# RWKV recurrence and MoE block: weight staging in one tile, and low parts and two products moved to GpSimd

## The chip, the core and the metric

One core of one Trainium2 chip runs the whole kernel in one launch. The metric is the device time of an execution in microseconds (us), shown as the median of several runs. Beside the runs stands one profiled execution of the kernel, from which all durations below are taken.

## What is computed

The reference runs a linear recurrence over 768 time steps for 4 x 8 heads of width 40, and then a two-layer block over the 3072 tokens that come out of it:

```python
for t in range(S):
    y[:, :, t] = einsum('bhd,bhde->bhe', rt, state)
    Sa = einsum('bhde,bhe->bhd', state, at)
    state = state * wt[:, :, None, :] - einsum('bhd,bhe->bhde', Sa, bt)
    state = state + einsum('bhd,bhe->bhde', vt, kt)
x = y.transpose(0, 2, 1, 3).reshape(B * S, H * D)      # 3072 x 320
h = x @ w_in                                           # 320 x 2048
g = where(h >= 1, h, where(h <= -1, 0, (h + 1) ** 2 / 4))
out = g @ w_out                                        # 2048 x 320
```

All inputs and outputs are fp32.

## The kernel before

**The recurrence.** Time is cut into 24 chunks of 32 steps, and six sets of four chunks. Per set the kernel forms the running products of w, their reciprocals (`rec`), and from them a, b and k scaled by these; it stores the scaled rows to a scratch in DRAM and reads them back per chunk in another layout. Each chunk has a 32 x 32 triangular matrix per head; its inverse is made for a whole set at a time by 31 elimination steps of two instructions each (`invert`, L362 and L368). Set 0's steps run on VectorE, those of the later sets on GpSimd. With the inverse at hand, `chain` carries the state from chunk to chunk through a fixed series: products on TensorE (L516, L526, L542, L553, L582), small scalings of their results on VectorE (L533, L560, L565, L584) and copies out of PSUM on ScalarE (L520, L537, L547).

**The start.** Sets 0 and 1 are prepared by `early_rows` (L164 to L193). For set 1 the inputs w, a, b and k are loaded early into tiles that later serve other ends: w into X0, a into X1, b into `tiab`, k into Y. X0 and X1 are also the tiles in which the tokens of the two-layer block will stand (in rows, X and X_92, X_93). `early_turn` transposes the rows of `at` (j = 0) and then of `bt` (j = 1) on TensorE in four parts each, `early_evict` copies them out of PSUM on ScalarE (L216), and `early_ab` (L227) makes the products from which set 1's triangular matrices come. PSUM has four rotating buffers for all of this and for the chain.

**The weights.** w_in comes as 12 pieces (jobs 0 to 11, tiles w_00 to w_32 of 120 or 80 rows by 512 columns), w_out as 16 pieces (128 x 320). They lie in DRAM as 8-byte words, of which this code rebuilds fp32 and splits it into a high and a low part. A job has these steps: raw loads queued on GpSimd (L708); two ScalarE passes, one that makes the upper bits in a place x (L720) and one that makes the lowest bits in a place `low` (L724); a VectorE pass that joins them in x (L728); then, one step later in the generator, the rounded high part on ScalarE (L740), and the low part as the difference of x and the high part (L741), on VectorE for w_in and on GpSimd for w_out. Each third piece of w_in also issues two copies on GpSimd (L746), and every split queues the raw load of five jobs on. x and `low` of the w_in jobs are thirds of X1 and of X0, taken in turn:

```python
x, low = (y[0:m, n * ((k + 1) % 3) :][:, 0:n] for y in (Xraw[1], Xraw[0]))
...
nc.scalar.copy(hi, x)
(nc.gpsimd if kind else nc.vector).tensor_sub(lo, x, hi.bitcast(F32))
```

**What sets the order.** The schedule is manual: each engine runs its instructions in the order in which the program text issues them, and the order is fixed by the code (`fill`, `feed`, `background`, and the list `steps` for set 1). An instruction that waits holds everything behind it on its engine. DMAs issued on SyncE and on GpSimd stand in these queues as well.

**The two-layer block** (`moe`) runs in twelve groups of 64 time steps as soon as `relayout` has moved the tokens from Y to X0 or X1 by DMA (L602 to L611). Per step: 16 products of 120 x 256 (L628), a gate (L636, L637 on ScalarE, L639 on VectorE), a split of the gate's result into a high part (L645, ScalarE) and a low part (L646, GpSimd), and 12 products (L658).

Of the kernel before, what the change touches and what calls it, by code (L numbers as in the profile page):

```python
# [9 lines left out]
F32 = mybir.dt.float32  # L10
# [44 lines left out]
def rwkv_moe_kernel(ctx: ExitStack, tc: tile.TileContext, r, k, v, w, a, b, w_in, w_out, ident_d, mask_d, out):  # L55
    nc = tc.nc
# [38 lines left out]
    Xraw = [x_tile(i, F32).rearrange("p c n -> p (c n)") for i in range(2)]  # L95
# [71 lines left out]
    def early_rows(s):  # L167


        wl, al, bl, kl = early_in[s]  # L170
        R = early_out[s]
        kt, P, at, bt = (R[:, :, D * i : D * i + D] for i in range(4))
        rec = arena[:, 0 : L * D].rearrange("p (t e) -> p t e", e=D)
        seg = lambda x: x.rearrange("p (s t) e -> p s t e", t=8)
        Ps, ws, rs = seg(P), seg(wl), seg(rec)
        nc.vector.tensor_copy(Ps[:, 1:, 0], ws[:, 1:, 0])
        nc.vector.tensor_scalar(out=P[:, 0], in0=wl[:, 0], scalar1=-1.0, scalar2=None, op0=ALU.mult)
        for t in range(1, 8):
            nc.vector.tensor_mul(Ps[:, :, t], Ps[:, :, t - 1], ws[:, :, t])
        for i in range(1, 4):  # L180
            nc.vector.tensor_mul(Ps[:, i], Ps[:, i], Ps[:, i - 1, 7:8].broadcast_to([128, 8, D]))
        yield
        nc.vector.tensor_scalar(out=at[:, 0], in0=al[:, 0], scalar1=-1.0, scalar2=None, op0=ALU.mult)
        nc.vector.tensor_mul(at[:, 1:], al[:, 1:], P[:, 0 : L - 1])
        yield
        nc.vector.reciprocal(rs[:, :, 7], Ps[:, :, 7])
        for t in range(7, 0, -1):
            nc.vector.tensor_mul(rs[:, :, t - 1], rs[:, :, t], ws[:, :, t])
        yield
        nc.vector.tensor_mul(bt, bl, rec)  # L190
        yield
        nc.vector.tensor_mul(kt, kl, rec)
        yield  # L193

    def early_turn(s, j, part):
# [499 lines left out]
    def weight_tile(k, t):  # L695
        kind, j, i, _ = jobs[k]
        if kind:
            if w2_pool[j // 8 ^ 1] is None:
                open_w2(j // 8 ^ 1)
            return w2_pool[j // 8 ^ 1].tile([128, 2, 320], t, name=f"w2_{j}", tag=f"w2_{j}")  # L700
        return w1_tile(j, i, t)

    def raw_load(k):
        raws[k] = weight_tile(k, F32).rearrange("p b n -> p (b n)")
        x, at = raws[k].bitcast(I32), 0
        for src in jobs[k][3]:
            m = src.shape[0]
            nc.gpsimd.dma_start(x[at : at + m], src.bitcast(I32))  # L708
            at += m

    def weights():

        def start(k):
            m, n = sizes[k]
            words = raws[k][0:m]
            if jobs[k][0]:
                x, low = Xraw[1][0:m, n * ((k + 2) % 3) :][:, 0:n], Xraw[1][0:m, 3 * n : 4 * n]
            else:
                x, low = (y[0:m, n * ((k + 1) % 3) :][:, 0:n] for y in (Xraw[1], Xraw[0]))
            nc.scalar.activation(  # L720
                x, words.rearrange("p (n b) -> p n b", b=2)[:, :, 1], AF.Prelu, scale=2.0**-112, alpha=2.0**32
            )
            low = low.bitcast(U32)
            nc.scalar.activation(  # L724
                low, words.bitcast(U8).rearrange("p (n b) -> p n b", b=8)[:, :, 3], AF.Copy, bias=-15.5 / 32, scale=1.0 / 32
            )
            yield
            nc.vector.scalar_tensor_tensor(  # L728
                out=x.bitcast(U32), in0=x.bitcast(U32), scalar=3, in1=low,
                op0=ALU.logical_shift_left, op1=ALU.bitwise_or,  # L730
            )
            yield x

        def split(k, x):
            m, n = sizes[k]
            kind, j, i, _ = jobs[k]
            del raws[k]
            wt[kind, j, i] = new = weight_tile(k, F32R)
            hi, lo = (new[0:m, p] for p in range(2))
            nc.scalar.copy(hi, x)  # L740
            (nc.gpsimd if kind else nc.vector).tensor_sub(lo, x, hi.bitcast(F32))  # L741
            converted[0] = k + 1
            if (kind, i) == (0, 2):
                wb = new.bitcast(F32)
                for q in range(2):
                    nc.gpsimd.dma_start(wb[80:120, q], wb[40 * q : 40 * q + 40, 0])  # L746
            if k + AHEAD < len(jobs):
                raw_load(k + AHEAD)

        late = None  # L750
        for k in range(len(jobs)):
            s = start(k)
            next(s)
            yield
            if late:
                split(*late)
            yield
            late = k, next(s)
            yield
        split(*late)  # L760

    def pull(gen, n=1):
# [25 lines left out]
    for i in range(2):  # L788
        init_cg(i, 2)
    rows_of = [early_rows(s) for s in range(2)]  # L790
    for j in range(2):
        for _ in range(2):
# [32 lines left out]
    i = 0  # L825
# [139 lines left out]
```

## Time and profile before

| | |
|---|---|
| runs, us | 864.71, 864.89, 858.93; median 864.71 |
| profiled execution, first to last instruction | 859.4 us |
| TensorE matmul busy | 690.8 us (80%) |
| VectorE busy | 594.3 us (69%) |
| ScalarE busy | 417.5 us (49%) |
| GpSimd busy | 441.8 us (51%) |
| moved by DMA | 122.01 MB |

The profiled execution lies between the runs: its span is 5.3 us under their median and 0.5 us over the fastest. In the rows, PE is the TensorE matmul, DVE is VectorE, ACT is ScalarE, POOL is GpSimd and SP is SyncE. L with a number is a line of the kernel. A letter q behind an engine (SPq) is its instruction queue. "x8" counts instructions that a row merges, and a square bracket tells how long the engine sat idle before the row and what ended that.

### The profile page before, as it was taken

What the parts mean: (1) busy time and instruction counts of PE and PEld (TensorE: products, weight loads), DVE (VectorE), ACT (ScalarE), POOL (GpSimd) and SP (SyncE); (2) the same over time, 40 slices, a digit from 0 to 9 for tenths busy, and PEclk for the clock granted to TensorE, in tenths of its full rate; (3) what the DMA queues carried; (4) which work ended last, traced back from release to release, by engine and by line L of the source; (5) the groups of instructions that cost most, each with busy time, mean ns of one, the idle gap of its engine ahead of it and who ended that gap; (6) DMA issues with size and microseconds to landing.
All of it is one profiled execution on the core that took longest, in us unless ns stands there. A gap on an engine that the chain in (4) does not pass through costs nothing.

```text
span 859.4 us, 35431 instructions
## 1 busy us (share of the span) xinstructions
PE 690.8 (80%) x15360; PEld 633.3 (74%) x15360; DVE 594.3 (69%) x1338; ACT 417.5 (49%) x888; POOL 441.8 (51%) x621
## 2 busy tenths in 40 slices
PE   4225656687567877878998889999999999999994
PEld 4224545576456866768887789898898999999994
DVE  6895689888556845787677797677876778676210
ACT  6306455557433533445545455455455555555552
POOL 0300279986232677845678548674267742222331
PEclk9665656788786989879999799999999999999998
DMA  8999599987598666986858976667354456350100
GB/s 291 188 198 233 95 194 206 217 196 184 130 172 149 152 156 112 181 189 150 165 127 165 190 179 154 131 130 134 85 111 89 98 106 131 84 119 23 36 16 16
DMA packets 221459, 122.01 MB, mean 142 GB/s; under 512 B 142144, under 2 KB 214016, under 8 KB 221304
## 3 DMA queue, kind: packets, MB, share of 16 engines
q1 hardware_dynamic: 215032, 98.12, 56.6%
q0 software_dynamic: 6272, 21.63, 9.4%
q8 instruction: 121, 1.98, 1.1%
q14 instruction: 34, 0.28, 0.1%
HBM read 90.54 MB, written 27.53 MB: 137 GB/s over the span
## 4 chain that ended last, share of the span: by engine, by line
PE 42%; DMA 10%; DVE 6%; POOL 5%; ACT 3%; SPq 3%; issue 2%; ACTq 0%; DVEq 0%; POOLq 0%
PE ph L628 14%; PE po L658 13%; PE p L553 4%; DMA ti<-scr 3%; PE p L542 3%; SPq L313 3%; DMA tiab<-scr 2%; PE p L516 2%; PE p L582 2%; PE p L482 2%; PE p L526 2%; DMA ld_b<-in_b_dram 2%; DMA scr<-arena 2%; POOL gl L646 1%; POOL lw L368 1%
## 5 line engine op out<-in xcount | busy, mean ns | idle before, releaser
L646 POOL TENSOR_TENSOR gl<-gt,gh 128x512 fp32r<-128x512 f32 x96 | 123.8, 1290 | 204.5 <-ACT gh L645 204.5
L628 PE MATMUL ph<-X,w 120*128 120x256 f32 x1536 | 219.1, 296 | 1.2 <-issue 1.2
L628 PEld LDWEIGHTS ph<-X,w 120*128 120x128 f32 x1536 | 198.7, 198 | 8.3 <-issue 1.7
L658 PE MATMUL po<-w,gh 128*128 128x320 f32 x768 | 135.9, 320 | 19.8 <-ACT gh L645 19.8
L658 PEld LDWEIGHTS po<-w,gh 128*128 128x128 f32 x768 | 117.4, 193 | 23.8 <-ACT gh L645 23.1
L639 DVE SCALAR_TENSOR_TENSOR gt<-gt,ph 128x512 f32<-128x512 f32 x96 | 65.7, 684 | 96.2 <-ACT gt L637 87.2
L537 ACT ACTIVATE cg<-p 32x160 f32<-32x160 f32 x192 | 56.5, 295 | 92.5 <-PE p L526 58.8
L658 PE MATMUL po<-w,gl 128*128 128x320 f32 x384 | 79.7, 332 | 20.7 <-POOL gl L646 20.7
L560 DVE SCALAR_TENSOR_TENSOR cg<-p,pr 40x160 f32<-40x160 f32 x184 | 59.1, 321 | 50.8 <-PE p L553 48.7
L636 ACT ACTIVATE gt<-ph,half_c 128x512 f32<-128x512 f32 x96 | 66.0, 688 | 58.0 <-PE ph L628 58.0
L368 POOL TENSOR_TENSOR lw<-lw 128x31 f32<-128x31 f32 (+15 forms) x155 | 86.6, 559 | 9.4
L362 POOL TENSOR_TENSOR lw<-lw 128x31 f32<-128x31 f32 (+15 forms) x155 | 84.0, 542 | 8.9
L494 DVE TENSOR_TENSOR cg<-p,mask 32x256 f32<-32x256 f32 x192 | 80.6, 420 | 3.5
L658 PEld LDWEIGHTS po<-w,gl 128*128 128x128 f32 x384 | 63.7, 201 | 25.3 <-POOL gl L646 24.9
L553 PE MATMUL p<-cg 128*64 128x72 f32 (+1 forms) x1536 | 66.0, 245 | 0.0
L645 ACT CAST gh<-gt 128x512 fp32r<-128x512 f32 x96 | 59.6, 621 | 10.5 <-DVE gt L639 9.5
L547 ACT COPY ss<-p 40x320 f32<-40x320 f32 x92 | 38.6, 419 | 48.7 <-PE p L542 47.2
L637 ACT ACTIVATE gt<-gt 128x512 f32<-128x512 f32 x96 | 60.7, 632 | 3.1
L553 PEld LDWEIGHTS p<-cg 128*64 128x64 f32 x1536 | 60.4, 154 | 0.4 <-issue 0.4
L533 DVE SCALAR_TENSOR_TENSOR cg<-p,mask 32x128 f32<-32x128 f32 x192 | 55.3, 288 | 6.3 <-PE p L526 1.1
L582 PEld LDWEIGHTS p<-pr,ss 40*40 40x40 f32 x1472 | 35.9, 129 | 30.1 <-issue 23.1
L582 PE MATMUL p<-pr,ss 40*40 40x32 f32 x1472 | 40.9, 210 | 21.1 <-DVE pr L466 16.3
(94 smaller groups left out, 1058.9 us busy)
## 6 DMA issues: line engine op xcount, KB each, us to landing
ti<-scr SPq DMA_DIRECT2D x96, 200.0 KB
ti<-scr SPq DMA_DIRECT2D x96, 168.0 KB
scr<-arena POOLq DMA_DIRECT2D x16, 640.0 KB, 6.4
cg<-scr SPq DMA_DIRECT2D x96, 80.0 KB
X<-Y SPq DMA_DIRECT2D x36, 160.0 KB
scr<-wide SPq DMA_DIRECT2D x8, 640.0 KB
w<-in_moe_w_out_dram POOLq DMA_DIRECT2D x16, 320.0 KB, 5.2
tiab<-scr SPq DMA_DIRECT2D x32, 160.0 KB
```

Of the source, the lines that this page charges most:

```text
L362: eng.tensor_mul(t3, W3[:, 0:n, j : j + 1].broadcast_to([128, n, m]), L3[:, j + 1 :, j].unsqueeze(1).broadcast_to([128, n, m]),)
L368: eng.tensor_sub(W3[:, 0:n, j + 1 :], W3[:, 0:n, j + 1 :], t3)
L494: nc.vector.tensor_tensor(out=cg[q, f::2, C_X : C_X + 64][:, 4 * i : 4 * i + 4].rearrange("p h (j x) -> p h j x", x=32), in0=ps[quarter(f, ...
L553: nc.tensor.matmul(psv[h // 8][64 * f : 64 * f + 64, h // 2 % 4, 0:n3], lhsT=cgw[:, h * CW + C_G : h * CW + C_G + 64], rhs=cg[:, h, C_R : ...
L582: nc.tensor.matmul(psv[er[f], p, :], lhsT=ss[er[f], p, :], rhs=pn[er[f], p, 0, 8:40], start=True, stop=True)
L628: nc.tensor.matmul(phs[k % 2][:, n * j : n * j + n], lhsT=wt[0, f // 4, wi // 2][:, wi % 2, fs], rhs=Xs[g][:, xi, :], start=i == 0, stop=i ...
L636: nc.scalar.activation(gt, ph, AF.Relu, bias=half_c, scale=0.5)
L637: nc.scalar.activation(gt, gt, AF.Square)
L639: nc.vector.scalar_tensor_tensor(out=gt, in0=gt, scalar=1.0, in1=ph, op0=ALU.min, op1=ALU.max)
L645: nc.scalar.copy(gh, gt)
L646: nc.gpsimd.tensor_sub(gl, gt, gh.bitcast(F32))
L658: nc.tensor.matmul(pos[i], lhsT=x[:, ts_], rhs=w, start=q == 0 and k == 0, stop=end)
```

## The change

Three edits. First, the products `bt` and `kt` of set 1 (and only of set 1) are formed by GpSimd. Second, the w_in jobs take both x and `low` from X1: x alternates between its first and second third, and `low` is always the last third; X0 is no longer used for weights. Third, the low part of all weights, w_in too, is formed by GpSimd.

```diff
@@ early_rows
-        nc.vector.tensor_mul(bt, bl, rec)
+        eng = nc.gpsimd if s else nc.vector
+        eng.tensor_mul(bt, bl, rec)
         yield
-        nc.vector.tensor_mul(kt, kl, rec)
+        eng.tensor_mul(kt, kl, rec)
         yield
@@ weights / start
-                x, low = (y[0:m, n * ((k + 1) % 3) :][:, 0:n] for y in (Xraw[1], Xraw[0]))
+                x, low = (Xraw[1][0:m, n * i : n * i + n] for i in ((k + 1) % 2, 2))
@@ weights / split
-            (nc.gpsimd if kind else nc.vector).tensor_sub(lo, x, hi.bitcast(F32))
+            nc.gpsimd.tensor_sub(lo, x, hi.bitcast(F32))
```

Behind L190 each line number of the changed kernel is higher by one. The order on TensorE and SyncE is the same in both kernels, and on ScalarE only the place of `low` differs. VectorE's order loses fourteen instructions and GpSimd's gains them.

VectorE where set 1's reciprocals end (L188), in the program before. X_93 is X1, X_92 is X0, wide_100 is the tile of set 1's rows, arena holds `rec`, w_00 and w_01 are the first two pieces of w_in, cg and p belong to the chain:

```order
L188 TENSOR_TENSOR arena<-arena,X_92 128x4x40 x7
L190 TENSOR_TENSOR wide_100<-tiab,arena 128x32x40
L728 SCALAR_TENSOR_TENSOR X_93<-X_93,X_92 120x512
L192 TENSOR_TENSOR wide_100<-Y,arena 128x32x40
L741 TENSOR_TENSOR w_00_732<-X_93,w_00_732 120x512
L533 SCALAR_TENSOR_TENSOR cg_85<-p_738,mask 32x4x32 x2
```

The same place in the changed program:

```order
L188 TENSOR_TENSOR arena<-arena,X_92 128x4x40 x7
L729 SCALAR_TENSOR_TENSOR X_93<-X_93 120x512
L534 SCALAR_TENSOR_TENSOR cg_85<-p_738,mask 32x4x32 x2
L534 SCALAR_TENSOR_TENSOR cg_85<-p_739,mask 32x4x32 x2
L495 TENSOR_TENSOR cg_86<-p_764,mask 32x4x64 x4
```

The two products and the first difference are gone from in front of the chain's L533 (now L534); only one joining pass is left between the reciprocals and the chain.

GpSimd behind the first raw loads, in the program before (pr_90 is a tile that is cleared once the transposes have read it):

```order
L708 DMA w_11_506<-in_moe_w_in_dram 40x1024
L708 DMA w_12_735<-in_moe_w_in_dram 40x1024 x2
L708 DMA w_20_959<-in_moe_w_in_dram 80x1024
L708 DMA w_20_959<-in_moe_w_in_dram 40x1024
L131 MEMSET pr_90 128x16x8
```

The same place in the changed program:

```order
L709 DMA w_11_506<-in_moe_w_in_dram 40x1024
L191 ISA
L191 TENSOR_TENSOR wide_100<-tiab,arena 128x32x40
L193 TENSOR_TENSOR wide_100<-Y,arena 128x32x40
L742 TENSOR_TENSOR w_00_732<-X_93,w_00_732 120x512
L709 DMA w_12_735<-in_moe_w_in_dram 40x1024 x2
L742 TENSOR_TENSOR w_01_956<-X_93,w_01_956 120x512
L709 DMA w_20_959<-in_moe_w_in_dram 80x1024
L709 DMA w_20_959<-in_moe_w_in_dram 40x1024
L131 MEMSET pr_90 128x16x8
```

The raw loads of w_12 and w_20 now stand behind the products and behind the first differences.

GpSimd amid set 1's elimination steps (tile lw), before:

```order
L573 TENSOR_TENSOR Y<-yt,Y 128x2x4x32
L362 TENSOR_TENSOR lw<-lw 128x156
L708 DMA w_32_1418<-in_moe_w_in_dram 40x1024 x2
L368 TENSOR_TENSOR lw<-lw 128x6x26
L362 TENSOR_TENSOR lw<-lw 128x175
L708 DMA w_0_1433<-in_moe_w_out_dram 128x640
L368 TENSOR_TENSOR lw<-lw 128x7x25
```

The same stretch in the changed program:

```order
L574 TENSOR_TENSOR Y<-yt,Y 128x2x4x32
L363 TENSOR_TENSOR lw<-lw 128x156
L742 TENSOR_TENSOR w_20_1415<-X_93,w_20_1415 120x512
L709 DMA w_32_1418<-in_moe_w_in_dram 40x1024 x2
L369 TENSOR_TENSOR lw<-lw 128x6x26
L363 TENSOR_TENSOR lw<-lw 128x175
L742 TENSOR_TENSOR w_21_1426<-X_93,w_21_1426 120x512
L709 DMA w_0_1433<-in_moe_w_out_dram 128x640
L369 TENSOR_TENSOR lw<-lw 128x7x25
```

Each difference of w_in stands ahead of the raw load that its split queues, between elimination steps.

## Rows read from the trace of the kernel before

**Rows 1.** Timeline of ACT, 47 to 84 us: start, us, instruction, idle before.

```profile
47.05 0.68 ACT L720 ACTIVATE X<-w 120x512 f32<-120x512 f32 x1
...
67.61 0.67 ACT L724 ACTIVATE X<-w 120x512 uint32<-120x512 uint8 x1 [19.89 <-DVE arena L188]
68.19 4.73 ACT L216 COPY wide<-p 40x512 f32<-40x512 f32 x8
...
82.80 1.18 ACT L216 COPY wide<-p 40x512 f32<-40x512 f32 x2
```

**Rows 2.** Timeline of DVE, 27 to 76 us.

```profile
27.68 1.45 DVE L184 TENSOR_TENSOR wide<-X,wide 128x1240 f32<-128x1240 f32 x1
...
65.10 2.48 DVE L188 TENSOR_TENSOR arena<-arena,X 128x160 f32<-128x160 f32 x7
67.62 1.49 DVE L190 TENSOR_TENSOR wide<-tiab,arena 128x1280 f32<-128x1280 f32 x1
69.03 0.69 DVE L728 SCALAR_TENSOR_TENSOR X<-X,X 120x512 uint32<-120x512 uint32 x1
...
74.72 0.69 DVE L741 TENSOR_TENSOR w<-X,w 120x512 fp32r<-120x512 f32 x1 [3.60 <-ACT w L740]
75.42 1.21 DVE L533 SCALAR_TENSOR_TENSOR cg<-p,mask 32x128 f32<-32x128 f32 x4
```

**Rows 3.** Windows: length, busy us (count) of each engine, clock, DMA share, GB/s.

```profile
82.90:97.25 14.35, 9.11 (x384) 8.36 (x384) 5.12 (x11) 5.90 (x12) 0.00 (x0) 0.64 0.28 30
...
111.52:145.38 33.86, 21.88 (x640) 19.70 (x632) 30.24 (x67) 18.07 (x43) 31.23 (x50) 0.60 1.08 191
145.38:163.22 17.84, 13.11 (x274) 11.71 (x266) 17.26 (x39) 11.70 (x28) 17.22 (x23) 0.80 0.98 218
```

**Rows 4.** Waits of 150 to 185 us: who waited for whom, total, times, longest.

```profile
PE po L658 <- POOL gl L646: 8.3, 2, 6.4
...
ACT arena L279 <- DMA scr<-arena: 4.9, 1, 4.9
```

**Rows 5.** Waits of SyncE's queue, 20 to 240 us.

```profile
SPq L602 <- POOL w L741: 7.3, 1, 7.3
```

**Rows 6.** Windows of 100 us.

```profile
500.00:600.00 100.00, 95.77 (x2333) 87.66 (x2332) 77.98 (x186) 51.92 (x116) 66.01 (x96) 1.00 0.68 145
```

**Rows 7.** Instruction groups by form, POOL, 0 to 240 us: busy, mean ns, idle.

```profile
L741 POOL TENSOR_TENSOR w<-X,w 128x320 fp32r<-128x320 f32 x16 | 15.4, 965 | 5.3 <-ACT w L740 5.2
...
L646 POOL TENSOR_TENSOR gl<-gt,gh 128x512 fp32r<-128x512 f32 x7 | 9.1, 1294 | 4.7 <-ACT gh L645 4.7
```

**Rows 8.** Timeline of PE at 76 us.

```profile
76.69 4.82 PE L203 MATMUL p<-pr,wide 128*40 128x64 f32 x96 [0.92 <-ACT cg L537]
```

**Rows 9.** Timeline of POOL, 111 to 164 us.

```profile
111.52 1.07 POOL L746 DMA_DIRECT2D w<-w  x2 [7.59 <-ACT w L740]
...
120.09 0.95 POOL L368 TENSOR_TENSOR lw<-lw 128x175 f32<-128x175 f32 x1
121.12 0.52 POOL L362 TENSOR_TENSOR lw<-lw 128x192 f32<-128x192 f32 x1
...
145.38 0.86 POOL L741 TENSOR_TENSOR w<-X,w 128x320 fp32r<-128x320 f32 x1 [0.45 <-ACT w L740]
...
163.22 1.04 POOL L296 TENSOR_TENSOR arena<-ld_b,wz 128x320 f32<-128x320 f32 x1
```

**Rows 10.** DVE's differences (L741) alone, 98 to 140 us: busy of DVE and POOL.

```profile
98.00:140.00 42.00, 7.55 (x10) 0.00 (x0) 0.62 1.08 196
```

**Rows 11.** Waits of 100 to 150 us.

```profile
DVE w L741 <- ACT w L740: 3.6, 5, 0.7
```

**Rows 12.** Timeline of DVE at 178 us.

```profile
178.42 3.57 DVE L728 SCALAR_TENSOR_TENSOR X<-X 128x320 uint32<-128x320 uint32 x1
```

**Rows 13.** Timeline of POOL at 180 us.

```profile
180.59 1.04 POOL L296 TENSOR_TENSOR arena<-ld_b,wz 128x320 f32<-128x320 f32 x1
```

**Rows 14.** Timeline of SyncE's queue, 34 to 50 us.

```profile
34.77 14.66 SPq L235 DMA_DIRECT2D scr<-wide  x3
```

## The prediction

> **What bounds the kernel now.** I read three views, from coarse to fine: the busy time by stretch, the waits of the stretches that the change touches, and the timelines there. Late in the run TensorE is the bound: of the 100 us from 500 on it computes 95.77 [rows 6], in an order that the program fixes. A microsecond won or lost earlier therefore moves the end by about as much, as long as nothing else becomes late. The change acts earlier, on jobs 0 to 11 of the weights and on set 1, so I follow 47 to 163 us.
>
> At 47.05 ScalarE makes x of job 0, and then sits 19.89 us in front of the pass for `low` [rows 1]. It waits for VectorE's L188, the last reader of set 1's w, because that w lies in X0 where `low` is to go. Eight evictions of set 1's transposes wait behind it and run from 68.19 [rows 1]. They hold PSUM buffers that the chain needs, and ScalarE's high part of job 0 stands behind them too, so VectorE waits 3.60 us before L741, and its chain instruction L533 begins at 75.42 only [rows 2].
>
> Later another engine decides. From 82.90 to 97.25 GpSimd does nothing; from 111.52 to 145.38 it is busy 31.23 of 33.86 us, with VectorE close behind at 30.24, and then 17.22 of 17.84 up to 163.22 [rows 3]. The second stretch begins with the copies of w_12 after 7.59 us of idling, and at 145.38 GpSimd again waits 0.45 us for ScalarE [rows 9]: until there it just keeps pace with the others. After that they wait for it. Its L296 at 163.22 [rows 9] goes into a store, and ScalarE waits 4.9 us for that store to land, while TensorE waits 6.4 us for GpSimd's L646 [rows 4]. At the weights' end SyncE's queue waits 7.3 us for GpSimd's last difference before it can move tokens into X1 [rows 5]. So I take GpSimd's arrival at L296 as what passes on to the end.
>
> **The start, edits one and two.** The reader sees in [rows 2] that a, which lay in X1, is last read by L184, over at 29.1 (27.68 + 1.45). `low` of job 0 thus finds its place free at 47.7, and the evictions are done before 67 us instead of at 72.9. VectorE ends L188 at 67.58 (65.10 + 2.48) in either kernel, then has one joining pass (0.69) and reaches the chain at 68.3 instead of 75.42: 7.1 us earlier on that engine. The wait on ScalarE doesn't vanish, though. There is one `low` now, so job 1's may be written only after job 0's joining pass, at 68.3. That is late by little, since the evictions no longer stand behind it.
>
> What comes next is `bt`, which the second transposes need. VectorE did it in 1.49 us [rows 2]; no row has it on GpSimd. The nearest row is L646, 1294 ns for 512 columns [rows 7]: 3.24 us in proportion to 1280 columns. The other bound goes by the engines' ratio for a difference, 1294 ns over VectorE's 0.69 us for the same width [rows 2, 7], a factor of 1.88, so 2.8 us. I take 3.0. The ISA entry that moves in front of it has no row; it falls before 67 us, where GpSimd waits anyway. [...]
>
> If GpSimd starts when L188 ends or up to one joining pass later, `bt` is there at about 71.0. TensorE's four parts are 128 products at 4.82 us for 96 [rows 8]: 6.4 us, until 77.4. ScalarE has its first part at 72.6, and four evictions of 1.18 and the two passes of a weight job (0.68 and 0.67) [rows 1] take it to 78.7. Before, they were over at 83.98 (82.80 + 1.18) [rows 1]. The products for set 1 (L227) stand behind them. The start is worth **-5.3 us**. `kt` follows on GpSimd until 74; only the stores of set 1's rows wait for it, which are read back for chunks 4 to 7.
>
> **From 79 us to the copies of w_12.** VectorE loses the differences of w_02, w_10 and w_11: three of 0.69 [rows 2], with about 0.7 of waiting, as the mean of the waits in [rows 11]: 2.8 us. Against it stands a new wait. x has two places instead of three, so the x of job k+1 overwrites that of job k-1, whose difference GpSimd must have formed. On ScalarE that x pass often stands right behind the high part of k-1. There it waits a whole difference, 1.3 us [rows 7], at w_11 and w_12: 2.6 us. Behind it stand the copies of the chain. The two sums cancel, and w_12's own difference comes ahead of its copies. I take the copies of w_12 at 106.5 instead of 111.52, **5.0 us earlier**. The differences up to here lie in GpSimd's idle stretches, 14.35 us [rows 3] and 7.59 us [rows 9]; without that cover each would cost its 1.3.
>
> **From the copies of w_12 to L296.** Here there is no cover. Before, GpSimd takes 51.70 us (111.52 to 163.22) [rows 9]. Added are six differences, w_20 to w_32, at 1.29 [rows 7]: +7.7 (the other bound: at the mixed mean of the 320-column ones, 965 ns scaled to 512 columns, 1.54 each and +9.3). Taken away is what VectorE's own differences cost it: an elimination step that met one took 0.95, its larger neighbour 0.52 [rows 9]. Five such at 0.4 give 2.0 (bounds 0 and 2.8). ScalarE and GpSimd wait for each other in turn now, which may leave GpSimd idle; I put 0.3 (bounds 0 and 1.0). Together 51.7 + 7.7 - 2.0 + 0.3 = 57.7, and L296 starts at 106.5 + 57.7 = 164.2 instead of 163.22: **+1.0 us**. VectorE, relieved of 7.55 us in 98 to 140 [rows 10], gets ahead and then waits. The raw loads of w_12 and w_20 now stand behind the two products, so from about 75 on. I cost that at nothing: their jobs' last steps come at 106.5 and later, and only a landing of some 20 us would be seen.
>
> So the sum is 859.4 + 1.0 = 860.4 us for the profiled execution. Its span lies 5.3 us under the median of the runs, 864.71, so for the median I say 865.7.
>
> **Rivals.** *Faster: VectorE is the bound from 98 to 140, not GpSimd.* For it speaks how near the two are, 30.24 to 31.23 [rows 3], and that VectorE waits 3.6 us for high parts there [rows 11]. Then 7.55 [rows 10] and 3.6 come on top of the start: 859.4 - 5.3 - 7.55 - 3.6 = 843.0, or 848.3 as a median. Against it: GpSimd has 2.63 us of room in that stretch [rows 3] and gets 7.7. This rival passes 1% (8.6 us) if 3.3 us beside the start's 5.3 survive, so if GpSimd can slip by that much without anyone waiting. I give 0.18 to faster by over 1%.
>
> *Slower: GpSimd holds VectorE off.* In the trace one joining pass, from 178.42, takes 3.57 us instead of 0.69, and ends at 181.99, just behind GpSimd's L296, which is over at 181.63 [rows 2, 12, 13]. At 67.6 the joining pass of job 0 and `bt` start together. If `bt` gets in first, and `kt` follows without a gap, VectorE comes through at 73.7 and not at 67.6: the start's gain falls to 1.2 us (the evictions end at 82.8), a price of 4.1. In the crowded stretch the same collisions stretch differences and steps: 9.3 instead of 7.7, and the 2.0 not given back, since the joining passes stay: 3.6. With the 4.1 that is 7.7: 859.4 + 1.0 + 7.7 = 868.1, or 873.4 as a median, just past 1%. It decides if both parts come whole; the start's part alone stays inside. [...] I let VectorE be first, as in [rows 2] it starts 0.04 us behind L188 on its own engine without any message between engines. I give 0.16 to slower by over 1%.
>
> *The change doesn't do what it says:* the single `low` brings ScalarE's wait back at job 1, again until L188 and the joining pass. If the evictions also waited, for instance for the stores that read the same tile, the start would give nothing: 859.4 + 1.0 + 5.3 = 865.7, or 871.0 as a median. The stores are issued by 49.4 (34.77 + 14.66) [rows 14], 18 us ahead of L188's end, so I leave this little, inside the 0.66 below.
>
> **Chances.** The forecast, the start's gain eaten by GpSimd, and its neighbours within 1% hold 0.66; faster by over 1% 0.18, slower 0.16. One per cent is about what a measurement of this kernel tells from no change. The forecast alone, with its bounds (GpSimd's differences, what is given back, the lock at the start), runs from 863 to 874; the faster rival takes the range's lower end to 853, where half of its gain beyond the start is had.
>
> **What would show it.** Right: no idle of 19.89 us before ScalarE's `low` of job 0; the first L534 at about 68.3; set 1's L227 (then L228) at about 79; L747 of w_12 at about 106.5; GpSimd without gaps from there to L296 (then L297) at about 164; ScalarE waiting for GpSimd before its x passes. Wrong: L297 before 160 us, the differences on GpSimd well under 1.29 us, or idle time on GpSimd between 107 and 163; or a joining pass of job 0 that ends after 71.

## The result, and the profile after

| | before | after |
|---|---|---|
| median of the runs, us | 861.38 (17 runs, 857.4 to 864.89) | 866.82 (17 runs, 859.92 to 873.82) |
| ratio, 95% interval | | 1.0058, 1.0038 to 1.0077 |
| a second set of runs of both | 859.79 (25 runs) | 863.83 (10 runs), ratio 1.0029, 1.0007 to 1.0051 |
| profiled executions, span, us | 859.4 | 870.9; in the second set 859.8 |

The changed kernel is slower by 0.3 to 0.6%; both intervals leave 1 out, and both lie within the 1% that the prediction called no change. One of its first 17 runs (873.82) was in the slow state and is left out of the ratio. The 865.7 that was forecast is 0.1% below the first median and 0.2% above the second. The working behind it is another matter: the copies of w_12, which end one step of it, came 7.1 us later than forecast in the first trace and 4.6 us in the second, and what happened there is the subject of most experiments. The first profiled execution of the changed kernel is a long one (872.65 us against the median of 866.82). Its granted clock, as a share of full speed, is 0.95 from 500 to 600 us and 0.98 from 700 to 800, where the kernel before has 1.00, and 0.867 in the mean, where the second execution has 0.884. So its end says little; I read it up to 171 us, and beside it the second one ("the repeat" below).

Page of the changed kernel: busy time of each engine with its share and its instructions, and the DMA queue that carries instructions (packets, MB, share):

```profile
span 870.9 us, 35421 instructions
...
PE 694.8 (80%) x15360; PEld 638.6 (73%) x15360; DVE 584.8 (67%) x1324; ACT 417.9 (48%) x888; POOL 461.8 (53%) x635
...
q8 instruction: 121, 1.98, 1.0%
```

VectorE has lost 9.5 us and GpSimd gained 20.0, as the change says. Now the places of the prediction, in order of time. The timeline of ScalarE (start us, us, instruction, idle before and what ended it):

```profile
53.26 4.75 ACT L217 COPY wide<-p 40x512 f32<-40x512 f32 x8 [5.47 <-DMA scr<-wide]
...
67.98 0.67 ACT L725 ACTIVATE X<-w 120x512 uint32<-120x512 uint8 x1 [9.28 <-DVE X L729]
...
78.57 1.18 ACT L217 COPY wide<-p 40x512 f32<-40x512 f32 x2
...
88.50 0.58 ACT L232 COPY pairs<-p 128x512 f32<-128x512 f32 x1 [5.61 <-PE p L228]
94.02 0.85 ACT L548 COPY ss<-p 40x320 f32<-40x320 f32 x2 [4.94 <-PE p L543]
...
100.45 0.68 ACT L721 ACTIVATE X<-w 120x512 f32<-120x512 f32 x1 [1.39 <-POOL w L742]
```

The 19.89 us in front of job 0's `low` [rows 1] are gone, and the first eight evictions run at 53 instead of 68. They did wait, 5.47 us, for the stores that read the same tile, as the prediction's last rival feared; it cost nothing, since `bt` comes only later. Job 1's `low` waits 9.28 us for job 0's joining pass, which was expected to be harmless and is. The second set of evictions ends at 79.75 (78.57 + 1.18) instead of 83.98 [rows 1]. Then ScalarE waits twice for TensorE, 5.61 and 4.94 us. Behind them, 1.39 us for a GpSimd difference in front of an x pass: the new wait of the prediction. VectorE and GpSimd at the start:

```profile
67.26 0.68 DVE L729 SCALAR_TENSOR_TENSOR X<-X 120x512 uint32<-120x512 uint32 x1
67.98 0.58 DVE L534 SCALAR_TENSOR_TENSOR cg<-p,mask 32x128 f32<-32x128 f32 x2
...
73.09 1.02 DVE L729 SCALAR_TENSOR_TENSOR X<-X 120x512 uint32<-120x512 uint32 x1
```

```profile
67.43 3.27 POOL L191 TENSOR_TENSOR wide<-tiab,arena 128x1280 f32<-128x1280 f32 x1 [28.56 <-DVE arena L188]
70.67 2.90 POOL L193 TENSOR_TENSOR wide<-Y,arena 128x1280 f32<-128x1280 f32 x1
73.53 1.71 POOL L742 TENSOR_TENSOR w<-X,w 120x512 fp32r<-120x512 f32 x1
...
99.15 1.27 POOL L742 TENSOR_TENSOR w<-X,w 80x512 fp32r<-80x512 f32 x1 [12.59 <-ACT w L741]
...
113.63 1.07 POOL L747 DMA_DIRECT2D w<-w  x2
...
170.65 1.05 POOL L297 TENSOR_TENSOR arena<-ld_b,wz 128x320 f32<-128x320 f32 x1
```

The joining pass starts ahead of `bt` and takes 0.68 us: VectorE was not held off. The chain's L534 comes at 67.98 (75.42 before [rows 2]). But the copies of w_12 stand at 113.63 where the prediction had 106.5, and L297 at 170.65 where it had 164.2. Between the two GpSimd is busy 53.49 of 57.02 us (columns as in [rows 3]):

```profile
113.63:170.65 57.02, 34.88 (x808) 31.12 (x808) 41.09 (x92) 28.61 (x66) 53.49 (x81) 0.58 0.87 179
```

So the copies of w_12 were 2.1 us late where 5.0 us early was forecast, after evictions that were 4.2 us early. What lies between is TensorE. Its timeline, before and then after:

```profile
84.04 2.13 PE L227 MATMUL p<-wide 40*32 40x32 f32 x147 [0.36 <-ACT wide L216]
87.83 1.70 PE L227 MATMUL p<-wide 40*32 40x32 f32 x107 [1.66 <-issue]
89.46 0.95 PE L542 MATMUL p<-cg 128*40 128x40 f32 x21
91.42 0.56 PE L542 MATMUL p<-cg 128*40 128x40 f32 x10 [1.00 <-issue]
```

```profile
79.80 2.23 PE L228 MATMUL p<-wide 40*32 40x32 f32 x147 [0.36 <-ACT wide L217]
86.75 1.70 PE L228 MATMUL p<-wide 40*32 40x32 f32 x107 [4.72 <-issue]
88.39 0.95 PE L543 MATMUL p<-cg 128*40 128x40 f32 x21
93.36 0.62 PE L543 MATMUL p<-cg 128*40 128x40 f32 x11 [4.02 <-issue]
```

The products that had been due at 84.04 are due at 79.80, and then TensorE stops twice, 4.72 and 4.02 us instead of 1.66 and 1.00. "Issue" means that it waits for nothing that the profile shows: no engine and no transfer of the program. The two stops are 128 products apart in both kernels (107 + 21), with their weight loads 256 instructions. That looks like the arrival of the next block of instructions, and the instruction queue of the page of the profile agrees with it: q8 moved 1.98 MB in 121 packets, 16.4 KB each, where TensorE's 15360 products with as many weight loads make 120 blocks of 256. One packet for 256 instructions is an estimate from these counts. DMA from 78 to 98 us (a digit is the busy share of half a microsecond in tenths), before and after:

```profile
DMA  9999999999999972200001000000010000000017
```

```profile
DMA  9989999999999999999999978820000010000000
```

In the changed kernel the DMA engines are full until 91 us, not until 85.5. The stores of set 1's rows (L236, four of 640 KB) start at 73.59 after and at 71.14 before, in the trace of SyncE.

### The profile page after: what moved, and what is told of

Its sections match the earlier page's. It is cut to its first block, busy times and chain, and to the rows that moved or that the text cites. A ratio compares the mean times of both kernels' runs of the same rounds, so it can differ in the third digit from the quotient of the medians.

```text
span 870.9 us, 35421 instructions
## 1 busy us (share of the span) xinstructions
PE 694.8 (80%) x15360; PEld 638.6 (73%) x15360; DVE 584.8 (67%) x1324; ACT 417.9 (48%) x888; POOL 461.8 (53%) x635
## 3 DMA queue, kind: packets, MB, share of 16 engines
q8 instruction: 121, 1.98, 1.0%
## 4 chain that ended last, share of the span: by engine, by line
PE 50%; DVE 14%; POOL 13%; DMA 8%; issue 6%; ACT 6%; SPq 3%; ACTq 0%; POOLq 0%; DVEq 0%
PE ph L629 15%; PE po L659 15%; PE p L554 4%; PE p L543 3%; POOL lw L369 3%; DMA tiab<-scr 3%; POOL lw L363 3%; DMA scr<-arena 3%; PE p L583 2%; PE p L517 2%; PE p L527 2%; PE p L483 2%; POOL w L742 2%; PE p L204 2%; POOL gl L647 2%
## 5 line engine op out<-in xcount | busy, mean ns | idle before, releaser
L629 PE MATMUL ph<-X,w 120*128 120x256 f32 x1536 | 224.5, 301 | 2.6 <-DMA X<-Y 1.3
L629 PEld LDWEIGHTS ph<-X,w 120*128 120x128 f32 x1536 | 203.4, 203 | 9.9 <-issue 3.1
L534 DVE SCALAR_TENSOR_TENSOR cg<-p,mask 32x128 f32<-32x128 f32 x192 | 55.3, 288 | 9.7 <-ACT cg L538 3.5
```

What stands on the lines that cost most here:

```text
L629: nc.tensor.matmul(phs[k % 2][:, n * j : n * j + n], lhsT=wt[0, f // 4, wi // 2][:, wi % 2, fs], rhs=Xs[g][:, xi, :], start=i == 0, stop=i ...
```

## The experiments

Theories. **F** (fetch): TensorE waits for its instructions behind other transfers, so whatever comes early at 80 us only waits longer. **G** (GpSimd): the six crowded differences and the new waits on ScalarE cost the rest. Rivals: the products of set 1 on GpSimd, or the later raw loads, are the whole loss. Edits are against the changed kernel unless said otherwise. The numbers of all runs stand in one table; each paragraph below draws on its row. "Before" in the last two columns are runs of the kernel before, taken together with those of the row; the ratio is not the quotient of the two medians, and where they differ (+3.94 us is 0.46%, the ratio of that row says 0.22%) the interval decides. "Stops" are TensorE's two waits for issue, "w_12" the start of its copies on GpSimd, "stretch" the time from there to L297. Executions of one kernel differ: between the two of the changed kernel L297 differs by 2.2 us and the span by 11.1, so of single traces only the stops and the stretch are read closely.

| kernel | stops, us | w_12 | L297 | stretch | median, minus before | ratio (95%) |
|---|---|---|---|---|---|---|
| before | 1.66 + 1.00 | 111.52 | 163.22 | 51.70 | | |
| changed | 4.72 + 4.02 | 113.63 | 170.65 | 57.02 | +5.44 | 1.0058 (1.0038 to 1.0077) |
| changed, the repeat | 5.37 + 2.92 | 111.10 | 168.45 | 57.35 | +4.04 | 1.0029 (1.0007 to 1.0051) |
| staging edit alone | 3.46 + 1.27 | 111.17 | 164.25 | 53.08 | -0.27 | 0.9991 (0.9960 to 1.0022) |
| differences of w_in on VectorE | 5.26 + 4.02 | 114.12 | 167.18 | 53.06 | +3.94 | 1.0022 (0.9991 to 1.0053) |
| differences of jobs 6 to 11 on VectorE | 5.35 + 4.84 | 113.96 | 167.09 | 53.13 | +0.33 | 1.0003 (0.9973 to 1.0032) |
| bt, kt on VectorE | 3.23 + 2.92 | 110.29 | 167.47 | 57.18 | +3.39 | 1.0045 (1.0017 to 1.0072) |
| raw loads early | 5.39 + 1.55 | 110.21 | 167.24 | 57.03 | +4.17 | 1.0039 (1.0009 to 1.0070) |
| copies of r and v late | 4.99 + 1.27 | 110.27 | 167.36 | 57.09 | +2.74 | 1.0036 (1.0013 to 1.0058) |
| before, raw loads late | 3.24 + 1.27 | 113.11 | 164.85 | 51.74 | +1.71 | 1.0016 (0.9986 to 1.0047) |
| half on VectorE, loads early, copies late | 5.17 + 1.00 | 110.02 | 163.63 | 53.61 | +0.42 | 1.0002 (0.9973 to 1.0030) |
| stores late | 1.08 + 1.27 | 107.23 | 165.31 | 58.08 | +2.97 | 1.0033 (1.0015 to 1.0051) |
| stores late, half on VectorE, loads early | 1.94 + 1.00 | 106.64 | 164.53 | 57.89 | +2.65 | 1.0027 (1.0006 to 1.0047) |
| the same, set 2's inputs first | 2.04 + 0.72 | 106.52 | 163.47 | 56.95 | +2.50 | 1.0035 (1.0015 to 1.0055) |

**The parts of the change, one by one.** The third edit undone, wholly and for the crowded half:

```diff
-            nc.gpsimd.tensor_sub(lo, x, hi.bitcast(F32))
+            (nc.gpsimd if kind else nc.vector).tensor_sub(lo, x, hi.bitcast(F32))
```

> The differences (low parts) of w_in are formed by VectorE again; the two products on GpSimd and the single tile for x and low stay. Theory A (GpSimd is full from the copies of w_12 to L297, so six differences there cost what they take): that stretch falls from 57.0 to about 52 us and the median from 866.8 to about 861.5. Theory B (at 82 to 94 us TensorE sits without its next instructions because the DMA engines are busy; 4.7 and 4.0 us against 1.7 and 1.0 before): it is untouched by this edit, so both gaps stay at 4 us or more. Rival C (not GpSimd's work but ScalarE's waiting for an x place, of which there are two, costs the time): the waits move to VectorE and the median stays within 2 us of 866.8.

```diff
-            nc.gpsimd.tensor_sub(lo, x, hi.bitcast(F32))
+            (nc.vector if 6 <= k < 12 else nc.gpsimd).tensor_sub(lo, x, hi.bitcast(F32))
```

> Of the twelve differences of w_in the first six (w_00 to w_12) stay on GpSimd and the last six (w_20 to w_32) go back to VectorE. Theory A: the first six lie in idle time of GpSimd, so this gives as much back as moving all twelve: about 52 us from the copies of w_12 to L297 and a median of about 861.5, within 1.5 us of the run that moves all twelve. If the first six cost too (about 1.3 us each at ScalarE's x passes), it stays 2 to 4 us above that run. Theory B: the gaps at 82 to 94 us stay at 4 us or more.

Either one brings the stretch down from 57.0 to 53.1 us. GpSimd's timeline with all differences of w_in back on VectorE:

```profile
114.12 1.07 POOL L747 DMA_DIRECT2D w<-w  x2 [7.60 <-ACT w L741]
128.93 1.05 POOL L747 DMA_DIRECT2D w<-w  x2 [1.02 <-ACT w L741]
142.74 1.07 POOL L747 DMA_DIRECT2D w<-w  x2 [0.73 <-ACT w L741]
...
167.18 1.05 POOL L297 TENSOR_TENSOR arena<-ld_b,wz 128x320 f32<-128x320 f32 x1
```

So the six crowded differences cost 3.9 us here, and the early ones next to nothing, as they lie in idle time. In the medians the two kernels don't agree that well, +3.94 and +0.33 us, where 861.5 was expected for both; their intervals overlap, so the runs don't decide whether the early six cost something further on. The 1.4 us that remain over the 51.70 of [rows 9] are the staging's: GpSimd waits 1.02 and 0.73 us for high parts that come later on ScalarE, where the same copies wait 0 and 0.35 us in the kernel before. The stops on TensorE stay as they are, so theory G isn't the whole.

The first edit undone, and then the first and third (the staging alone is left):

```diff
-        eng = nc.gpsimd if s else nc.vector
+        eng = nc.vector
```

> The two products of set 1 on VectorE again; the differences on GpSimd and the single tile stay. The raw loads of w_12 and w_20 are queued early again by themselves, and set 1's stores start some 3 us earlier. Theory B: the gaps on TensorE at 80 to 94 us fall to 5 us or less in total, L561 comes at 90 to 93. VectorE's chain instruction L534 comes 3 us later, at about 71. Theory A: the stretch from the copies of w_12 to L297 stays at about 57 us. Both together: a median of about 863. Neither gap nor stretch depends on the products if it is rival C alone: then 866 or more.

> Only the single tile for x and low; products and differences on VectorE as before. ScalarE's evictions come early, and VectorE's chain instruction L534 at about 73 instead of 75.4. Theory B: TensorE reaches its fetch some 2 to 4 us earlier, when the DMA engines are still busy, so its gaps grow by about as much as was gained and L561 stays near 92 to 93. Theory A: 52 to 53 us from the copies of w_12 to L297. Together within 2 us of the kernel before. If x's two places matter by themselves, 3 us or more slower.

With the products back on VectorE the chain's L534 stands at 70.84 and the stores start at 70.84 in place of 73.59; the first stop falls to 3.23 us. That fits F: stores that are issued earlier are done earlier. The raw loads of w_12 come earlier here too (71.93 instead of 75.19), so the run doesn't tell the two apart. The stretch is unchanged at 57.2, as G has it. The staging alone costs and gains nothing that can be measured (0.9991), though its evictions end at 80.33 (79.14 + 1.19), 3.65 us earlier than before: the first stop has grown by 1.8 and the stretch by 1.4.

**Transfers around 80 us.** The raw loads of w_12 and w_20 early again; the copies of r and v (L142) eight slices of work later, which moves r's from 78.39 to 100.18 us and leaves v's at about 100; and, from the other side, the kernel before with its raw loads as late as in the changed one (the third diff is against the kernel before):

```diff
-    for k in range(AHEAD):
+    for k in range(AHEAD + 2):
...
-            if k + AHEAD < len(jobs):
+            if k > 1 and k + AHEAD < len(jobs):
```

> The changed kernel with the raw loads of w_12 and w_20 queued with the first ones again, ahead of the two products on GpSimd. Theory B: 480 KB less has to be moved from 75 to 91 us, the DMA engines are free by about 88, the two gaps on TensorE fall from 8.7 us to 5 or less, L561 comes at about 92 instead of 95, and the median at about 863.5. Theory A alone: nothing changes before 110 us and the median stays at 866.8. The stretch from the copies of w_12 to L297 stays at 57 us in both.

```diff
-    steps += [[lambda i=i: copy_rv(1, i, 0, 4)] for i in range(2)] + [[lambda: pad_scr(1)]]
+    steps += [[] for _ in range(8)] + [[lambda i=i: copy_rv(1, i, 0, 4)] for i in range(2)] + [[lambda: pad_scr(1)]]
```

> The changed kernel with one thing moved: the copy of set 1's r into the scratch (640 KB in pieces of 160 bytes) is queued behind the next chunk's loads, so some 20 us later. Theory B (TensorE's gaps at 80 to 94 us are its instruction fetch behind busy DMA engines): the DMA engines fall idle by about 83, both gaps shrink to about 1.7 and 1 us, L561 comes at about 89 instead of 95, and the copies of w_12 at about 108 instead of 113.6. If the gaps are not from DMA traffic they stay at 4 to 5 us. Both r and v copies then stand ahead of the next loads on SyncE's queue, which may hold those up by some us after 100; so I expect a median of 860 to 865 rather than the full 6 us off 866.8.

```diff
-    ... [[lambda: init_cg(2, 2)]]
+    ... [[lambda: (init_cg(2, 2), raw_load(5), raw_load(6))]]
...
-            if k + AHEAD < len(jobs):
+            if k > 1 and k + AHEAD < len(jobs):
```

> The kernel before with nothing changed but the place of the raw loads of w_12 and w_20: behind the clearing of pr_90 on GpSimd, at about 82 us instead of 40 to 43. Theory B: these 480 KB are then moved in the very stretch in which TensorE fetches (84 to 92), the two gaps grow from 1.7 and 1.0 us to 3 or more each, L560 moves from 93.1 to 96 or later, and the median by +3 to +5 us. If DMA traffic has nothing to do with the gaps: L560 at 93, median unchanged.

Either of the first two shrinks the second stop, from 4.02 us (2.92 in the repeat) to 1.55 and 1.27, and leaves the first at 5. Neither brings the median back (+4.17 and +2.74): the raw loads aren't the whole loss, nor were the products (+3.39 without them). In the kernel before, the same loads at 81 us lengthen the first stop from 1.66 to 3.24: transfers whose data nobody waited for yet did hold TensorE up there. The second stop, expected at 3 us or more, stays at 1.27, and the median's +1.71 is within its noise. Both repairs and the half on VectorE together:

> The changed kernel with three repairs: the last six differences of w_in on VectorE, the raw loads of w_12 and w_20 early, the copy of set 1's r late. Theories A and B together: 4 us from the first (57 to 53 from the copies of w_12 to L297), 3 to 6 us from the other two, so the copies of w_12 at 105 to 108, L297 at 158 to 161, and a median 3 to 6 us under the kernel before. If the late copy only moves the traffic in front of the next chunks' loads, the gain is given back there and it lands at the time of before.

The two repairs don't add, since they cure the same second stop; w_12 is at 110.0 to 110.3 with either or both. The stretch is 53.6, as expected. The copies of w_12 and L297 miss the 105 to 108 and 158 to 161 that were expected; L297 and the median are those of the kernel before.

**The first stop.** Left are the stores. They move behind the next chunk's loads on SyncE, twelve slices of work on and spread:

```diff
-    steps += [[lambda c=c: early_store(1, c)] for c in range(4)]
+    steps += [[] for _ in range(12)]
+    for c in range(4):
+        steps += [[lambda c=c: early_store(1, c)]] + [[] for _ in range(3)]
```

> The changed kernel with one thing moved: the four stores of set 1's rows (L236, issued from SyncE at about 74) come twelve and more slices of work later, spread over them, and the copies of r and v move with them. If TensorE's first wait for its next instructions (4.7 us at 82) is due to these stores' traffic, it falls to about 1.5 us, L228 goes on at about 82.5, L561 stands at about 88.5, the copies of w_12 at about 107 and L297 at about 163.5; the median is then some 4 to 7 us under the changed kernel's, 860 to 863. If the wait has to do with the instructions themselves and not with other transfers, it stays at 4.5 to 5.5 us, L228 goes on at 85 to 87 as in all runs so far, and L561 stays at 91 to 95. If the stores are merely late for chunks 4 to 7, the place of the wait moves behind 96 and L297 stands at 167 or later.

Timeline of TensorE and DMA from 78 to 98 us of this kernel:

```profile
80.00 2.23 PE L228 MATMUL p<-wide 40*32 40x32 f32 x147 [0.36 <-ACT wide L217]
83.32 1.70 PE L228 MATMUL p<-wide 40*32 40x32 f32 x107 [1.08 <-issue]
84.95 0.95 PE L543 MATMUL p<-cg 128*40 128x40 f32 x21
87.18 0.56 PE L543 MATMUL p<-cg 128*40 128x40 f32 x10 [1.27 <-issue]
```

```profile
DMA  0000010000000103978320000000005999799999
```

The products start at the same 80.0 us as in the changed kernel, the DMA engines are idle, and the stop is 1.08 instead of 4.72 us. Same instructions, same order on TensorE, other traffic: that TensorE's wait hangs on the other transfers is shown. That what it waits for are its instructions can be read from the packets of the instruction queue. Queue q8 in a window that holds the second stop's packet, 88.9 to 90.2 us before and 90.8 to 92.0 us in the changed kernel (packets, MB, share):

```profile
q8 instruction: 1, 0.02, 5.8%
```

```profile
q8 instruction: 1, 0.02, 5.7%
```

Before, that one packet is moved from 88.94 to 90.14 and TensorE goes on at 91.42; in the changed kernel, from 90.89 to 91.99 and 93.36. So it is in all 14 traces: at each of the 28 stops TensorE goes on 1.2 to 1.6 us after a packet of 16 KB on q8 has landed. What differs is when the packet starts. The second stop's starts 1.1 us after TensorE went on from the first before (88.94 - 87.83), and 4.1 us after it in the changed kernel (90.89 - 86.75). Over the 14 traces it is 1.1 to 1.6 us where that stop lasts 0.7 to 1.6, and 2.8 to 4.6 where it lasts 2.9 to 4.8. This is what theory F says: in the changed kernel the packet stands behind other transfers and TensorE behind the packet.

The copies of w_12 come at 107.23, close to the 106.5 of the prediction. The stretch is 58.08, about 1 us longer, so L297 is 3.1 us earlier than in the repeat; the median, taken on the same chip as the repeat's, is only 1.1 lower. With the crowded half on VectorE and the raw loads early as well:

> As the kernel with late stores, and also the differences of jobs 6 to 11 on VectorE and the raw loads of w_12 and w_20 with the first ones. If the stores' traffic made TensorE's waits and the six crowded differences made the rest, both are gone: copies of w_12 at about 107, L297 at about 160, and a median 2 to 5 us under the kernel before. If the first wait has another cause, it stays near 5 us, L297 stands at about 163.5 and the median is within 1 us of the kernel before.

I expected L297 at 160 here. It came at 164.53, with a stretch of 57.89 where 53.6 was due. Timeline of ScalarE, and of GpSimd, in that kernel:

```profile
151.78 0.75 ACT L270 COPY wz<-ld_w 128x320 f32<-128x320 f32 x1 [7.27 <-DMA ld_w<-in_w_dram]
```

```profile
153.64 1.21 POOL L281 TENSOR_TENSOR arena<-ld_a,ld_w 128x320 f32<-128x320 f32 x1 [5.92 <-DVE ld_w L246]
```

Set 2's first w is late, since SyncE issues it behind the moved stores and copies, at 146.04 instead of 141.48 in the row "half on VectorE, loads early, copies late". The last run starts set 2's loads ahead of the stores, with the same order on the other engines:

```diff
-    steps += [[] for _ in range(12)]
+    steps += [[] for _ in range(12)] + [[lambda: spent.setdefault(("rows", 2), [next(back["rows"])])]]
```

> As the kernel with late stores, half of the differences on VectorE and early raw loads, and also the first loads of set 2's w, a and k (ld_w, L262) moved on SyncE's queue from behind set 1's late stores and copies to ahead of them; the order on the other engines is the same. If that queue is where the 7 us won by the free instruction fetch were given back, GpSimd's 5.9 us in front of L281 and ScalarE's 7.3 us for ld_w are gone, the copies of w_12 are again at about 106.6, L297 is at 159 to 160.5, and the median is 2 to 4 us under the kernel before (ratio 0.995 to 0.998). If what counts is the amount of traffic in 96 to 145 and not the place in the queue, other waits of 4 to 6 us for ti loads or for X<-Y take the place of that one, L297 is at 163 to 165 and the ratio within 0.3% of 1.

The wait for ld_w is gone, and L297 comes at 163.47: the second of the two expectations (its ratio, 1.0035, a little beyond it). The longest waits of 107 to 166 us are now for the tokens of the block (who waited for whom, total, times, longest):

```profile
ACT Y L573 <- DMA X<-Y: 9.1, 1, 9.1
...
PE ph L629 <- DMA X<-Y: 8.6, 1, 8.6
```

ScalarE's is new; it was 0.5 us in the kernel before this one. TensorE's was there already, with 8.3 us. So the 4 to 7 us that a free fetch wins at 107 were not kept in these three kernels: with the stores' 2.6 MB and the copies in a later place, set 2's inputs or the tokens came late. That the traffic as such delays them is the likely reading, and not shown. Whether smaller stores, or stores on another queue, would do better wasn't tried. No version is faster than the kernel before by more than can be measured.

**The changed kernel once more.**

> The changed kernel once more, unaltered, for its trace. If the two waits of TensorE between 80 and 94 belong to the kernel and not to the one execution that was profiled, they are again 4 to 5.5 and 3.5 to 5 us long, the copies of w_12 stand at 113 to 114.5 and L297 at 170 to 171.5. If they were chance, their sum is under 6 us and L297 stands before 168. Its ratio to the kernel before is again 1.004 to 1.008 if that was measured rightly.

The stops are again 8.3 us in sum, and the stretch 57.35; w_12 and L297 came 2.5 and 2.2 us earlier than in the first trace, so between the two expectations; the second stop (2.92) and the ratio (1.0029) are also below what was expected. The stops and the stretch belong to the kernel; some 2 us of the place at 113.63 were that execution's.

## Why the prediction was right or wrong

**The start, -5.3: right, if a little high.** Evictions end at 79.75, 4.2 us earlier, and at 78.66 (77.47 + 1.19), 5.3 earlier, in the repeat. `bt` took 3.27 us (taken 3.0, the upper bound 3.24), `kt` 2.90. The lower bound, 2.8 by the ratio of the two engines for a difference, is too low for both, though for `bt` the first 0.5 us lie beside VectorE's joining pass, which may have held it. VectorE came first at 67.26 and took 0.68 us (0.69 before [rows 2]), so what the forecast calls the lock at the start did not occur. L534 stands at 67.98; 68.3 was forecast.

**79 us to the copies of w_12: the step that failed.** The prediction let its 5.3 us pass through to "106.5 instead of 111.52". It weighed ScalarE, VectorE and GpSimd there, and took TensorE's products as if they ran when their data came. From the evictions' end to ScalarE's next copy of the chain (L520, L521 in the changed kernel) it took 10.96 us before (83.98 to 94.94) and 17.29 after (79.75 to 97.04). The difference is 6.3, and the stops have grown by 6.1 (8.74 - 2.66). The 1.66 and 1.00 were there to be read in the trace of before, marked "issue", and I passed over them. The part that was worked out with care did come out: from L521 (L520) to the copies of w_12 it takes 16.59 us after and 16.58 before, so the saved differences and the waits in front of the x passes (1.39 and 1.38, taken as 1.3 each) cancel, though the 2.8 us for the former counts one wait of 0.7 for three differences.

**Raw loads "at nothing": wrong in kind.** I asked when their data would be missed, and not what their traffic would delay. Early loads leave 1.55 us of the second stop, 2.5 less than in the changed kernel and 1.4 less than in its repeat, and late ones put 1.6 us on the first stop of the kernel before.

**The copies of w_12 to L296: right.** 57.02 and 57.35 us against 57.7. The sum of the prediction was 7.7 - 2.0 + 0.3 = +6.0; measured is +5.3, of it +5.04 busy time of GpSimd (53.49 after, 48.45 before in the same stretch) and +0.28 idle. Six differences at 1.26 to 1.27 are 7.6, so about 2.5 were given back, between the 2.0 taken and the bound of 2.8. Undoing the differences returns only 3.9, since GpSimd then waits for ScalarE instead.

**L296 passes on to the end: only in part.** The changed kernel's first trace keeps its +7.4 (6.8 to 8.1 at the first 15 such instructions) until 500 us; the repeat starts with +5.2, has +2.7 at the third such instruction, +0.1 at the last, and ends 0.4 us behind before. Over the table, L297 and medians go together loosely: +0.2 to +2.1 us with -0.3 to +3.0, +3.9 to +4.3 with +0.3 to +4.2, and +5.2 to +7.4 with +4.0 and +5.4. The granted clock differs between single traces as well (from 145 to 165 us 0.81 before and 0.50 in the first of the changed kernel; over the stretch 0.67 before, 0.58 and 0.61 in the two of the changed kernel); how much of the looseness is its doing, no run separates. Against before, the forecast was +1.0 and the runs say +5.4 and +4.0. That 865.7 was nearly met all the same is luck in part: it stood on the median of three runs, 864.71, which is 3.3 us above that of the 17.

One place where 2.5 us are given back is the joining pass behind 178 us. Timeline of VectorE, of the changed kernel and then of the repeat:

```profile
185.72 3.71 DVE L729 SCALAR_TENSOR_TENSOR X<-X 128x320 uint32<-128x320 uint32 x1
```

```profile
183.14 0.49 DVE L729 SCALAR_TENSOR_TENSOR X<-X 128x320 uint32<-128x320 uint32 x1
184.25 3.02 DVE L729 SCALAR_TENSOR_TENSOR X<-X 128x320 uint32<-128x320 uint32 x1 [0.61 <-ACT X L725]
```

In the first it takes 3.71 us, as before 3.57 [rows 12]; in the repeat this pass comes through in 0.49 and only the next one is long, 3.02. From the second to the third L297 it is 14.92 us in the former and 12.34 in the latter. That the two belong together is read from these traces, not tested.

**Rivals.** Faster: refuted. VectorE, relieved, waits more: it is busy 41.09 of the 57.02 us, where it was 47.50 of 51.70; GpSimd, at 53.49, has no room to slip. Slower, with GpSimd holding VectorE off at 67.6: that didn't occur, the joining pass took 0.68 us there; how long it would have been held (until 73.7 in the prediction) was the author's estimate from the one row of 3.57 us. The change doesn't do what it says: the wait of 19.89 us did vanish, and the evictions' wait for the stores was harmless. Yet the start's gain was lost, as in that rival, by a cause that the prediction did not have: 163.22 + 1.0 + 5.3 is 169.5 for L297, and 170.65 and 168.45 were measured. Its median of 871.0 was not reached.

## What to carry to other kernels

A gain in one engine's arrival counts only if the next engine can start: look in the profile for waits of that engine that are put down to "issue", ask what the DMA engines carry at that moment, and expect that such a wait may grow when the work comes earlier and the traffic does not: here the products were due 4.2 us earlier and the first stop went from 1.66 to 4.72 us. Transfers had a price here even when nobody waited for their data: with the raw loads late, the first stop of the kernel before went from 1.66 to 3.24 us, and with the stores late, SyncE issued the next set's first w behind them and ScalarE waited 7.27 us for it. And where an engine has no idle time in a stretch, its busy time there can be added up: that sum came out within 1 us (57.7 against 57.02).

## What was not expected of the hardware

By the packets of q8, TensorE ran out of instructions here where many small products follow each other: 128 of them, with 128 weight loads, take 2.65 us (1.70 + 0.95), and from one stop's end to the next it is 3.59 us before (87.83 to 91.42), although almost nothing else is moved then (0 or 1 in the DMA row). The stops last 0.7 to 2.0 us in the three kernels with late stores, and up to 5.4 us where the DMA engines are full. In the nine traces with early products and with the stores issued from 70 to 75 us, TensorE goes on from the first stop at 84.9 to 86.8 us, whether it had stopped at 80.2 or at 82.3. A joining pass of VectorE took 3.0 to 3.7 us where it otherwise takes 0.49; in the changed kernel it ran from 185.72 to 189.43 while GpSimd went through four instructions without a gap (185.85 to 189.07), the longest 1.26 us, and ended 0.36 us behind the last. That is more than waiting for the one instruction of GpSimd that the prediction names beside it, L296 with its 1.04 us [rows 13]. That GpSimd held the pass is read from this overlap, not tested. Shorter meetings went with longer times too: the difference of job 0 took 1.71 us on GpSimd (otherwise 1.27) and the joining pass beside it 1.02 (otherwise 0.68). Whether each waited for the other in turn, or both were slower, isn't shown.
